# Tokens of a chunk side by side in memory, and a clamp of the weights' high words moved from VectorE to GpSimd

## The chip, the cores and the metric

The kernel runs on one core of a Trainium2 chip. The metric is the device time of one execution, in microseconds (us). The engines of the core work beside each other, each through its own instructions in their order: TensorE (PE) multiplies matrices, VectorE (DVE), ScalarE (ACT) and GpSimd (POOL) work element by element, and SyncE (SP) issues the transfers between memory (DRAM) and the on-chip memory. The tiles of the matrix unit's results lie in PSUM, all others in SBUF, on up to 128 partitions.

## The reference

Three layers in a row, on 12,480 tokens of 128 channels. Shapes are x (12480, 128), inducing (32, 128), each w_in (128, 2048) and each w_out (2048, 128).

```python
def mab(q, kv):
    s = scale * (q @ kv.T); a = softmax(s)
    return a @ kv
h = mab(inducing, x)               # 32 points look at all tokens
x = mab(x, h)                      # each token looks at the 32 points
hh = x @ w_in
x = (max(hh, 0) + alpha * min(hh, 0)) @ w_out
h = x @ w_in2
P = a0 + a1*h + a2*h**2 + a3*h**3
Q = 1 + |b0|*|h| + |b1|*h**2
out = (P / (Q + 1e-6)) @ w_out2
```

The four weight matrices come as float64, that is as pairs of 32-bit words, and are made into float32 on the chip. The tokens are independent of each other except in the sum over all tokens in h.

## The kernel before, in words

Tokens are taken in 104 tiles of 120 (one token a partition), 4 tiles to a chunk of 480 tokens (26 chunks), 4 chunks to a pack (7 packs, the last of 2 chunks). Token p * 104 + j is token p of tile j (lines 100 and 101), so that partition p of a load or a store takes one contiguous run, and the runs of neighbouring partitions lie 104 * 512 = 53,248 B apart.

**Loads.** load_x (line 155) brings a pack of x in transfers of 8 tiles each: 120 partitions, 4,096 B each, 480 KB, 13 transfers in all. load_w (line 162) brings half a float64 matrix, 1,024 KB, to 128 partitions: of w_in 8 KB of each row of 16 KB, of w_out 8 rows of 1 KB a partition. All are issued by SP in the order of lines 487 to 502: x packs 0 to 2, a half of w_in, x packs 3 and 4, a half of w_out, x packs 5 and 6, and the other weights. Halves of weights reuse the buffers of x's packs (slots), so SP waits until those are free.

**First part** (lines 520 to 600). For each pack: TensorE transposes the tiles (s1_t, line 262), scores against the inducing points (s1_s, with the maxima on VectorE, line 280), the exponential on ScalarE (s1_e), its transposition (s1_et) and the sum over the pack's tokens (s1_h). Behind the last pack the partial sums are brought under one maximum (gm, line 538) and give h and hT (line 599).

**Conversion of the weights.** Each matrix is cut into quarters of 128x512, 16 in all. For a quarter, cv_abs (line 200) takes the absolute value of the high words on ScalarE (line 203) into a tile cvt (3 buffers). Four steps on VectorE follow, which are queued in a list and taken out one by one: one (line 214: the clamp between LEAST and MOST), two (line 218: mask and shift), three (line 225: bits of the low word) and four (line 231: the sign and top bits; the result goes to its place). After four, a quarter of the first w_out is scaled on GpSimd (lines 184 and 187). Step one calls cv_abs itself if that has not been done. absn(n) issues cv_abs for the next n quarters, conv(n) the next n steps; CV (line 503) says how many of each stand in each pack's turn of the first part.

**Second part.** The order of all later operations is written out by hand: START (line 21) up to the sixth unit of the second layer, with "abs" for absn(1) and "cv" for conv(1) between the others, and CHUNK_ORDER (line 42) for every chunk after that. START carries the rest of the conversions beside the second softmax (s2_d, lines 402 and 403), the products with h (w_mm, w_hi, w_lo), the first layer's products (la, r, lb) and, on GpSimd, a_norm (422), a_lo (464) and w2_lo (327). From "close" on, units of the second layer run: products L690 to L692, then the rational function on ScalarE (s, z, rho, r0), VectorE (m 715, z 731, e 766, g0 770, g 774) and GpSimd (A 705, B 710, P 726).

**Stores.** out_y (line 808) copies a chunk's result and issues its store from SP, 240 KB, the last chunk's in two halves (27 in all).

Of the kernel before, what the change touches and what calls it, by code (L numbers as in the profile page):

```python
# [17 lines left out]

# The order in which the operations are issued, by their names in OPS: up to the second layer's
# sixth unit, and then for every chunk, with units, chunks and packs counted from the chunk's own.  # L20
START = """
# [44 lines left out]
def tile_induced_attention__prelu_moe__rational_moe(  # L66
# [13 lines left out]
    nc = tc.nc  # L80
# [4 lines left out]
    P = 128  # L85
    TP = 120                    # tokens of a tile: token = p * NT + tile
    NT = N // TP                # 104 tiles
    CH = 4                      # tiles of a chunk
    W = CH * TP                 # 480 tokens of a chunk
    NC = NT // CH               # 26 chunks  # L90
    NF = F // P                 # 16 feed-forward tiles
    NU = NF // 2                # units of two tiles
    NG = (NC + 3) // 4          # packs of four chunks
    R = P // M                  # copies of the inducing points on the partitions
    scale = 1.0 / math.sqrt(C)
    QC = 1.0 + 1e-6
    LEAST = 2.0**-15            # float32 of the bits of the high words of 2**-127 ...
    MOST = struct.unpack("f", struct.pack("I", 0x47EFFFFF))[0]      # ... and of nearly 2**128

    xv = x[0].rearrange("(p j) c -> p j c", j=NT)  # L100
    ov = out.rearrange("(p j) c -> p j c", j=NT)

# [24 lines left out]
    qc = cst.tile([P, 1], F32, name="qc")  # L127
    w1 = cst.tile([P, NF, C], F32, name="w1")          # (1 - alpha) * w_out
    w2o = wp.tile([P, NF, C], F32, name="w2o")
# [18 lines left out]

    # ---------------------------------------------------------------- pieces of the first part
    XS, RAW, SC, E, ET = {}, {}, {}, {}, {}  # L150
# [4 lines left out]
    def load_x(g):  # L155
        n = CH * nch(g)
        pool = xsr if g < 4 else cvr if g < 6 else xsl
        XS[g] = pool.tile([P, n, C], F32, tag=f"xs{g}", name="xs")
        for k in range(0, n, 8):
            nc.sync.dma_start(out=XS[g][:TP, k : k + 8], in_=xv[:, 4 * CH * g + k : 4 * CH * g + k + 8])  # L160

    def load_w(key, dram, half, slot):
        """Half of a float64 matrix, as pairs of words."""
        pool = xsr if slot in range(4) else cvr if slot in (4, 5) else xsl
        raw = pool.tile([P, F], U32, tag=f"xs{slot}", name="raw")
        if dram.shape[0] == P:
            nc.sync.dma_start(out=raw, in_=dram[:, F * half : F * half + F])
        else:
            n = F // 2
            nc.sync.dma_start(  # L170
                out=raw.rearrange("p (t d) -> p t d", t=NF // 2),
                in_=dram[n * half : n * half + n].rearrange("(t p) d -> p t d", p=P),
            )
        for q in range(2):
            RAW[key, 2 * half + q] = raw[:, F // 2 * q : F // 2 * (q + 1)]

    # float64 words to float32: sign, exponent and 20 bits from the high word, 3 from the low;
    # the quarters of the four matrices in turn, an operation at a time
    todo, done = [], set()
# [20 lines left out]
    def cv_abs(piece):  # L200
        w = RAW.pop(piece).rearrange("p (f two) -> p f two", two=2)
        t = cvr.tile([P, 512], F32, tag="cvt", name="cvt", bufs=3)
        nc.scalar.activation(out=t, in_=w[:, :, 1].bitcast(F32), func=AF.Abs)
        ABS[piece] = t, w[:, :, 0], w[:, :, 1]

    def cv_steps(piece):
# [3 lines left out]
        def one():  # L210
            if piece not in ABS:
                absn(1)
            t = ABS[piece][0]
            nc.vector.tensor_scalar(out=t, in0=t, scalar1=LEAST, scalar2=MOST, op0=ALU.max, op1=ALU.min)

# [35 lines left out]
    def absn(n):  # L251
        """The first operation, on its own engine, of the next n quarters."""
        for _ in range(n):
            if order:
                cv_abs(order.pop(0))
# [73 lines left out]
    def g_t(q, pool, tag, copy=True):  # L329
        """w_in @ diag(alpha) @ w_out"""  # L330
        t = pool.tile([P, 512], F32, tag=tag, name="t")
        for i in range(4):
            f = 4 * q + i
            nc.tensor.transpose(t[:, i * P : (i + 1) * P], wi[:, f * P : (f + 1) * P], ident)
        WT[q] = t
        if copy:
            g_c(q)
# [12 lines left out]
    def split_stack(t, dst):  # L350
        """hi, hi, lo, lo of the four copies on the partitions."""
        nc.scalar.copy(dst, t)
        hb = P // 2
        nc.vector.tensor_tensor(out=dst[hb:], in0=t[hb:], in1=f32(dst[hb:]), op=ALU.subtract)
# [3 lines left out]
    def rows(g, lo, hi):  # L358
        """The second softmax of chunks lo ... hi of pack g."""
        n = CH * nch(g)  # L360
        v = att[:, 4 * CH * g : 4 * CH * g + n, :].rearrange("p (i j) m -> p i j m", i=CH)
        return v[:, :, lo:hi, :]

    def s2_sc(g, lo, pool, tag):
        """Second softmax of the tokens of pack g: scores, differences from the maxima, exponentials."""
        sc = pool.tile([P, 512], F32, tag=tag, name="sc2")
        for j in range(lo, nch(g)):
            nc.tensor.matmul(
                sc[M * (j - lo) : M * (j - lo) + M, :W], lhsT=hT[:, 0, :], rhs=xT[:, 4 * g + j, :], start=True, stop=True
            )  # L370
        SC2[g] = sc, lo
# [16 lines left out]
    def s2_sc0(pool, tag):  # L388
        """The scores of the first chunk, tokens on the partitions."""
        t = pool.tile([P, 512], F32, tag=tag, name="t2")  # L390
# [37 lines left out]
    def a_sum(g, steps):  # L428
        """The sums of pack g's probabilities, halving after halving."""
        if g not in SUM:  # L430
# [17 lines left out]
    def a_parts(g, part):  # L448
        """Of pack g, one chunk of the first pack or half of the tiles: probabilities, and their hi, lo, hi, lo."""
        n = CH * nch(g)  # L450
# [21 lines left out]
    def a_t(c, pool, tag):  # L472
        """Probabilities of chunk c, transposed: hi, lo, hi, lo on the partitions."""
        g, j = divmod(c, 4)
# [10 lines left out]

    # ---------------------------------------------------------------- first part
    nc.sync.dma_start(out=ind, in_=inducing)
# [46 lines left out]

    # the maxima of all tokens beside the last partial sums
    s1_s(NG - 1)
# [25 lines left out]

    # the packs' partial sums under one maximum
    nc.vector.tensor_copy(hps[:, :nl, C : C + 1], sums[:, :nl].unsqueeze(2))
# [29 lines left out]
    cs2 = ctx.enter_context(tc.tile_pool(name="cs2", bufs=1, side="left", reuse_waits="tile"))  # L594
    wst = cs2.tile([P, F], F32R, name="wst")           # h @ w_in: hi, hi, lo, lo
    mst = cs2.tile([P, C], F32R, name="mst")           # h @ w_in @ diag(alpha) @ w_out: hi, hi, lo, lo
    hT = cs2.tile([P, R, M], F32, name="hT")
    att = cs2.tile([TP, NT, M], F32, name="att")       # second softmax
    nc.vector.tensor_copy(hT, t[:, 0:M].unsqueeze(1).to_broadcast([P, R, M]))
# [5 lines left out]

    # ---------------------------------------------------------------- second part
    ph1 = ctx.enter_context(tc.tile_pool(name="ph1", bufs=1, space=PSUM, reuse_waits="tile"))
# [90 lines left out]
    def act_z(k):  # L698
        """|b0 h|, over h."""
        h = hs_[k][:, :, :W]  # L700
# [16 lines left out]
    def act_h(k):  # L717
        """A copy of h, for Pool to multiply."""
        Mm[k] = pools["ew"].tile([P, 2, W], F32, tag="m", name="m", bufs=4)
# [23 lines left out]
    def last_r0():  # L743
        """The last unit's, in SBUF, and its product on Pool."""
        k = NUN - 1
# [13 lines left out]
    def keep_warm(n):  # L759
        """Products for nothing under the last chunk, which has no first layer beside it: the clock stays up."""  # L760
        t = ph1.tile([P, 512], F32, tag="h1", name="warm")
# [26 lines left out]
    def halves(c):  # L788
        """A chunk's evacuations: in one piece, or the last one's shared by two engines."""
        if c < NC - 1:  # L790
# [17 lines left out]
    def out_y(c):  # L808
        t = outp.pop(c)[:TP].rearrange("p (i d) -> p i d", i=CH)
        y = pools["rp2"].tile([TP, CH, C], F32, tag="y", name="y", bufs=2)  # L810
        for copy, a, b in halves(c):
            copy(y[:, a:b], t[:, a:b])
            nc.sync.dma_start(out=ov[:, CH * c + a : CH * c + b, :], in_=y[:, a:b])

    # fill: the rest of the weights and the second attention under the first chunk's first layer
    GP[1] = pr0.tile([P, 2, 512], F32, tag="r0", name="gp")[:, 0, :]
# [154 lines left out]
```

## Time and profile before

| | |
|---|---|
| time, median of 3 runs | 1259.12 us (1257.58 to 1259.64) |
| span of the profiled execution | 1255.9 us |
| the profiled execution's own time | not among the figures given; the span lies 3.2 us under the median of the runs |
| busy: VectorE, TensorE, ScalarE, GpSimd | 1192.9, 1179.6, 1132.8, 1077.5 us |
| transfers of x | 13, 480 KB each |
| the clamp (L214) | 16 instructions, 7.0 us on VectorE |

The span runs from the first to the last instruction of the profiled execution; a run's time has in addition what lies around it. Busy time is the time in which an engine executes an instruction. In the rows, L214 is line 214 of the kernel, "out<-in" names the tiles, x8 says that eight equal instructions are merged in a row, and a bracket gives the idle time before an instruction and what ended it.

### The profile page before, as it was taken

What the parts mean: (1) busy time and instruction counts of PE and PEld (TensorE: products, weight loads), DVE (VectorE), ACT (ScalarE), POOL (GpSimd) and SP (SyncE); (2) the same over time, 40 slices, a digit from 0 to 9 for tenths busy, and PEclk for the clock granted to TensorE, in tenths of its full rate; (3) what the DMA queues carried; (4) which work ended last, traced back from release to release, by engine and by line L of the source; (5) the groups of instructions that cost most, each with busy time, mean ns of one, the idle gap of its engine ahead of it and who ended that gap; (6) DMA issues with size and microseconds to landing.
All of it is one profiled execution on the core that took longest, in us unless ns stands there. A gap on an engine that the chain in (4) does not pass through costs nothing.

```text
span 1255.9 us, 12626 instructions
## 1 busy us (share of the span) xinstructions
PE 1179.6 (94%) x4153; PEld 677.3 (54%) x4153; DVE 1192.9 (95%) x1164; ACT 1132.8 (90%) x1510; POOL 1077.5 (86%) x770
## 2 busy tenths in 40 slices
PE   6798899999999999999999999999999999999987
PEld 4454455555455555555555555555555555555543
DVE  2699999999999999999999999999999999999997
ACT  4568899999999999999999999999999999999984
POOL 0137899999999899999999998999998999999996
PEclk9999999999999999999999999999999999999999
DMA  9800000000000000000000000000000000000000
GB/s 228 246 1 0 1 8 8 0 9 9 1 8 9 8 1 8 9 1 9 9 8 1 8 9 2 7 8 9 1 8 8 5 4 8 8 1 9 8 9 8
DMA packets 10286, 22.01 MB, mean 18 GB/s; under 512 B 764, under 2 KB 5148, under 8 KB 9708
## 3 DMA queue, kind: packets, MB, share of 16 engines
q1 hardware_dynamic: 10220, 21.20, 6.2%
q8 instruction: 33, 0.54, 0.2%
q14 instruction: 33, 0.27, 0.1%
HBM read 14.80 MB, written 6.39 MB: 17 GB/s over the span
## 4 chain that ended last, share of the span: by engine, by line
POOL 38%; PE 29%; DVE 18%; issue 6%; ACT 6%; DMA 2%; SPq 0%; POOLq 0%; ACTq 0%; DVEq 0%
POOL m L726 16%; POOL a L705 9%; PE oa L786 9%; POOL b L710 8%; PE xa L649 8%; DVE z L766 4%; DVE r L770 4%; DVE z L731 3%; DVE m L715 3%; PE h L692 3%; POOL m L723 2%; PE h L636 2%; DMA xs<-in_x_dram 2%; PE h L690 2%; PE h L691 2%
## 5 line engine op out<-in xcount | busy, mean ns | idle before, releaser
L726 POOL TENSOR_TENSOR m<-m,b 128x960 f32<-128x960 f32 x208 | 468.1, 2251 | 4.0
L649 PE MATMUL xa<-r,w 128*128 128x480 f32 x832 | 385.4, 570 | 16.1 <-ACT o L798 15.3
L786 PE MATMUL oa<-g,w2o 128*128 128x480 f32 x832 | 378.6, 569 | 13.3 <-ACT xf L665 10.4
L705 POOL TENSOR_SCALAR a<-s,co 128x960 f32<-128x960 f32 x208 | 240.5, 1156 | 82.9 <-ACT s L696 81.0
L641 ACT ACTIVATE r<-h 128x480 f32<-128x480 f32 x416 | 237.2, 571 | 24.9 <-PE h L636 22.6
L731 DVE SCALAR_TENSOR_TENSOR z<-s,bab,h 128x960 f32<-128x960 f32 x208 | 251.0, 1207 | 0.0
L766 DVE SCALAR_TENSOR_TENSOR z<-z,r 128x960 f32<-128x960 f32 x208 | 239.7, 1152 | 8.8 <-ACT r L740 5.4
L710 POOL TENSOR_SCALAR b<-s,co 128x960 f32<-128x960 f32 x208 | 240.7, 1157 | 0.0
L735 ACT ACTIVATE rho<-z,qc 128x960 f32<-128x960 f32 x208 | 225.1, 1095 | 16.0 <-DVE z L731 15.5
L636 PE MATMUL h<-stk,wst 128*128 128x480 f32 x416 | 233.0, 561 | 6.9 <-ACT r L641 6.4
L770 DVE TENSOR_TENSOR r<-m,r 128x960 f32<-128x960 f32 x207 | 239.1, 1155 | 0.0
L774 DVE SCALAR_TENSOR_TENSOR g<-z,r 128x960 f32<-128x960 f32 x207 | 237.4, 1147 | 1.0
L690 PE MATMUL h<-xh,w2h 128*128 128x480 f32 x416 | 215.2, 517 | 8.7 <-DVE z L731 8.3
L701 ACT ACTIVATE h<-h,bab 128x960 f32<-128x960 f32 x208 | 214.8, 1033 | 6.3 <-DVE m L715 5.2
L715 DVE TENSOR_TENSOR m<-h,a 128x960 f32<-128x960 f32 x183 | 210.4, 1150 | 8.0 <-POOL a L705 7.5
L786 PEld LDWEIGHTS oa<-g,w2o 128*128 128x128 f32 x832 | 153.5, 189 | 115.8 <-issue 80.2
L649 PEld LDWEIGHTS xa<-r,w 128*128 128x128 f32 x832 | 153.3, 189 | 113.1 <-issue 70.0
L740 ACT ACTIVATE r<-rho 128x960 f32<-128x960 f32 x207 | 201.8, 975 | 5.0 <-DVE g L774 4.8
L696 ACT ACTIVATE s<-h 128x960 f32<-128x960 f32 x208 | 202.4, 973 | 3.2 <-PE h L692 2.3
L692 PE MATMUL h<-xl,w2h 128*128 128x480 f32 x416 | 161.1, 387 | 5.7 <-POOL xl L676 5.1
L691 PE MATMUL h<-xh,w2l 128*128 128x480 f32 x416 | 158.2, 380 | 0.0
L636 PEld LDWEIGHTS h<-stk,wst 128*128 128x128 f32 x416 | 78.4, 189 | 116.8 <-ACT r L641 69.4
(136 smaller groups left out, 825.3 us busy)
## 6 DMA issues: line engine op xcount, KB each, us to landing
xs<-in_x_dram SPq DMA_DIRECT2D x13, 480.0 KB, 14.1
out_dram<-y SPq DMA_DIRECT2D x25, 240.0 KB, 2.4
raw<-in_moe_w_in_dram SPq DMA_DIRECT2D x4, 1024.0 KB, 6.1
raw<-in_moe_w_out_dram SPq DMA_DIRECT2D x4, 1024.0 KB, 12.1
out_dram<-y SPq DMA_DIRECT2D x2, 120.0 KB, 1.8
ind<-in_inducing_dram SPq DMA_DIRECT2D x1, 16.0 KB, 1.5
c<-in_moe_a_dram SPq DMA_DIRECT2D x1, 0.0 KB
c<-in_moe_b_dram SPq DMA_DIRECT2D x1, 0.0 KB
```

Source lines behind the costliest of these rows:

```text
L636: nc.tensor.matmul(t[:, :W], lhsT=wst[:, f * P : (f + 1) * P], rhs=stk[c], start=True, stop=True)
L649: nc.tensor.matmul(xacc[c][:, :W], lhsT=w1[:, f, :], rhs=rls.pop((p, i)), start=f == 0, stop=False)
L690: nc.tensor.matmul(t, lhsT=w2h[:, sl], rhs=xh, start=True, stop=False)
L705: nc.gpsimd.tensor_scalar(out=a, in0=S[k], scalar1=co[:, 3:4], scalar2=co[:, 1:2], op0=ALU.mult, op1=ALU.add)
L710: nc.gpsimd.tensor_scalar(out=b, in0=S[k], scalar1=co[:, 2:3], scalar2=co[:, 0:1], op0=ALU.mult, op1=ALU.add)
L715: nc.vector.tensor_tensor(out=Mm[k], in0=hs_[k][:, :, :W], in1=A_.pop(k), op=ALU.mult)
L726: nc.gpsimd.tensor_tensor(out=Mm[k], in0=Mm[k], in1=B_.pop(k), op=ALU.add)
L731: nc.vector.scalar_tensor_tensor(out=Z[k], in0=S.pop(k), scalar=bab[:, 1:2], in1=z, op0=ALU.mult, op1=ALU.add)
L766: nc.vector.scalar_tensor_tensor(out=Z[k], in0=Z[k], scalar=QC, in1=R0[k][:, :, :W], op0=ALU.add, op1=ALU.mult)
L770: nc.vector.tensor_tensor(out=r, in0=Mm.pop(k), in1=r, op=ALU.mult)
L774: nc.vector.scalar_tensor_tensor(out=g, in0=Z.pop(k), scalar=2.0, in1=R0.pop(k)[:, :, :W], op0=ALU.subtract, op1=ALU.mult, reverse0=True)
L786: nc.tensor.matmul(oacc[c][:, :W], lhsT=w2o[:, f, :], rhs=(G[k] if i == 0 else G.pop(k))[:, i], start=f == 0, stop=f == NF - 1)
```

## The change

Two things change; comments are also taken out, which changes no line number of a statement ahead of line 155 and shifts later ones by a few.

First, chunk n, partition p, tile i is now token n * 480 + p * 4 + i: a chunk is one contiguous piece of x and of out. A load has the same 8 tiles, two chunks, so each partition gets two runs of 2,048 B. A store of a chunk writes 2,048 B a partition as before, now without gaps between the partitions.

Second, the clamp is issued on GpSimd in cv_abs, directly behind ScalarE's absolute value; step one issues nothing unless cv_abs is still to be done. START, CHUNK_ORDER and CV are unchanged.

```diff
-    xv = x[0].rearrange("(p j) c -> p j c", j=NT)
-    ov = out.rearrange("(p j) c -> p j c", j=NT)
+    xv = x[0].rearrange("(n p i) c -> p n (i c)", p=TP, i=CH)
+    ov = out.rearrange("(n p i) c -> p n i c", p=TP, i=CH)
...
         for k in range(0, n, 8):
-            nc.sync.dma_start(out=XS[g][:TP, k : k + 8], in_=xv[:, 4 * CH * g + k : 4 * CH * g + k + 8])
+            m = min(8, n - k) // CH
+            nc.sync.dma_start(
+                out=XS[g][:TP, k : k + CH * m].rearrange("p (n i) c -> p n (i c)", i=CH),
+                in_=xv[:, 4 * g + k // CH : 4 * g + k // CH + m],
+            )
...
         nc.scalar.activation(out=t, in_=w[:, :, 1].bitcast(F32), func=AF.Abs)
+        nc.gpsimd.tensor_scalar(out=t, in0=t, scalar1=LEAST, scalar2=MOST, op0=ALU.max, op1=ALU.min)
         ABS[piece] = t, w[:, :, 0], w[:, :, 1]
...
         def one():
             if piece not in ABS:
                 absn(1)
-            t = ABS[piece][0]
-            nc.vector.tensor_scalar(out=t, in0=t, scalar1=LEAST, scalar2=MOST, op0=ALU.max, op1=ALU.min)
...
-            nc.sync.dma_start(out=ov[:, CH * c + a : CH * c + b, :], in_=y[:, a:b])
+            nc.sync.dma_start(out=ov[:, c, a:b], in_=y[:, a:b])
```

## Rows read from the trace of the kernel before

**Rows 1.** Stretches of 10 us and the loop: window, length, engines' busy us (instructions), clock, DMA.
```profile
60.00:70.00 10.00, 9.49 (x53) 3.77 (x50) 9.57 (x18) 8.00 (x16) 2.38 (x2) 1.00 0.28 88
...
80.00:90.00 10.00, 10.00 (x50) 6.21 (x49) 9.20 (x17) 7.47 (x16) 1.05 (x1) 1.00 0.00 0
...
100.00:110.00 10.00, 7.98 (x25) 4.42 (x25) 9.93 (x10) 7.92 (x11) 9.67 (x6) 0.96 0.00 0
...
400.00:1200.00 800.00, 774.37 (x2493) 443.51 (x2491) 788.36 (x722) 760.09 (x991) 742.54 (x527) 1.00 0.02 6
```

**Rows 2.** Chain of waits of the first 190 us: start, length, what.
```profile
3.97 11.31 DMA xs<-in_x_dram
...
20.29 16.98 DMA xs<-in_x_dram
```

**Rows 3.** Timeline of TensorE while x comes in: start, length, instructions, idle before.
```profile
8.70 1.72 PE L268 MATMUL t<-ident,xs 120*128 120x120 f32 x8 [0.33 <-DMA xs<-in_x_dram]
...
15.42 1.01 PE L268 MATMUL t<-ident,xs 120*128 120x120 f32 x8 [1.11 <-DMA xs<-in_x_dram]
...
37.40 1.80 PE L268 MATMUL t<-ident,xs 120*128 120x120 f32 x8 [4.55 <-DMA xs<-in_x_dram]
```

**Rows 4.** Stretches of 2 us: x alone, w_in, cold clock, w_out; columns as in rows 1.
```profile
6.00:8.00 2.00, 1.49 (x8) 1.49 (x8) 0.00 (x0) 0.39 (x1) 0.00 (x0) 1.00 1.03 227
...
18.00:20.00 2.00, 1.79 (x40) 1.36 (x38) 0.96 (x3) 1.69 (x4) 0.00 (x0) 1.00 0.98 344
...
38.00:40.00 2.00, 2.00 (x14) 1.02 (x13) 0.00 (x0) 1.12 (x2) 0.00 (x0) 0.50 1.01 301
...
58.00:60.00 2.00, 2.00 (x12) 0.65 (x11) 1.47 (x6) 1.70 (x5) 0.00 (x0) 1.00 1.09 360
```

**Rows 5.** Timeline of all engines from 44 to 58 us.
```profile
48.11 1.32 POOL L187 TENSOR_TENSOR w<-w,wa 128x512 f32<-128x512 f32 x1
48.34 1.38 DVE L218 TENSOR_SCALAR cvt<-cvt 128x512 uint32<-128x512 uint32 x1
...
49.64 0.64 DVE L280 TENSOR_REDUCE mx<-sc 64x1 f32<-64x480 f32 x1
```

**Rows 6.** Timeline of TensorE, its gaps between 57 and 97 us.
```profile
64.38 0.49 PE L636 MATMUL h<-stk,wst 128*128 128x480 f32 x1 [0.44 <-ACT r L641]
...
78.27 0.62 PE L385 MATMUL t<-ident,ss 128*120 128x128 f32 x4 [1.34 <-DVE att L403]
```

**Rows 7.** Timeline of VectorE: the clamp on the path, a step two, the first z.
```profile
62.15 0.43 DVE L214 TENSOR_SCALAR cvt<-cvt 128x512 f32<-128x512 f32 x1
62.61 0.43 DVE L218 TENSOR_SCALAR cvt<-cvt 128x512 uint32<-128x512 uint32 x1
...
66.30 0.64 DVE L214 TENSOR_SCALAR cvt<-cvt 128x512 f32<-128x512 f32 x1
...
75.08 0.42 DVE L214 TENSOR_SCALAR cvt<-cvt 128x512 f32<-128x512 f32 x1
75.53 1.15 DVE L218 TENSOR_SCALAR cvt<-cvt 128x512 uint32<-128x512 uint32 x1
...
106.60 1.20 DVE L731 SCALAR_TENSOR_TENSOR z<-s,bab,h 128x960 f32<-128x960 f32 x1
```

**Rows 8.** DMA issues by line: KB each, us from issue to landing.
```profile
out_dram<-y SPq DMA_DIRECT2D x25, 240.0 KB, 2.4
...
out_dram<-y SPq DMA_DIRECT2D x2, 120.0 KB, 1.8
```

**Rows 9.** Groups by line, first 150 us: count, busy us, mean ns, idle before.
```profile
L218 DVE TENSOR_SCALAR cvt<-cvt 128x512 uint32<-128x512 uint32 x16 | 11.1, 694 | 0.5
...
L214 DVE TENSOR_SCALAR cvt<-cvt 128x512 f32<-128x512 f32 x16 | 7.0, 439 | 3.2 <-ACT cvt L203 3.1
...
L187 POOL TENSOR_TENSOR w<-w,wa 128x512 f32<-128x512 f32 x4 | 5.4, 1341 | 0.3
```

**Rows 10.** The page's costliest groups: GpSimd's one-input instruction.
```profile
L710 POOL TENSOR_SCALAR b<-s,co 128x960 f32<-128x960 f32 x208 | 240.7, 1157 | 0.0
```

## The prediction

> **What bounds the kernel now.** I read the table of stretches first, then the chain of waits, then the timelines of single engines where the chain stands. From 400 to 1200 us VectorE is busy 788.36 of 800 us, and TensorE, ScalarE and GpSimd are close behind [rows 1]: the chunk loop is bound by VectorE, and nothing in it is changed except the address of a store. So the change can act only ahead of the loop, in the first 110 us, and what it gains or loses there moves the end by as much, since the loop behind it has no slack to take it up. Those 110 us have four parts, and in each another thing ends last.
>
> Up to 37.4 us it is the load of x: the chain names it for 11.31 and then 16.98 us [rows 2]. The start of each eight transposes waits for one transfer of 480 KB, and from the second to the fifth they start from 8.70 to 15.42 [rows 3]: 6.72 us for three intervals, 2.24 us each, so 491,520 B / 2.24 us = 219 GB/s. The DMA engines are full meanwhile (share 1.03) at 227 GB/s, while with the weights alone they move 344 and 360 GB/s [rows 4].
>
> From 37 to 57 us it is a chain of small steps across TensorE, ScalarE and VectorE, and the reduction of L280 at 49.64 stands in it [rows 5].
>
> From 57 to 97 us VectorE and TensorE are both full: 9.57 of 10 us and 10.00 of 10 us [rows 1]. TensorE's larger gaps there are 0.44 and 1.34 us, the second until VectorE's L403 [rows 6].
>
> From 97 to 108 us VectorE is full again (9.93 of 10 [rows 1]) with the last conversions, and the first unit's z, at 106.60, comes behind them [rows 7].
>
> **The layout.** The bytes and the number of transfers stay (13 loads of x, 27 stores). In memory a partition's 4,096 B of a load become two pieces of 2,048 B, and the runs of neighbouring partitions, 53,248 B apart now, come to lie end to end. Does the gap cost something now? w_in has gaps too: a transfer takes 8 KB of each 16 KB row, and at 18 to 20 us it moves 344 GB/s; w_out is read in 1,024 B pieces without gaps, at 360 GB/s [rows 4]. So neither gaps nor small pieces slow a load that fills 128 partitions. What sets x apart is that it fills 120, and that stays. I put the gain at 0. The ends: at 344 GB/s a transfer takes 1.43 us, and the eleven that must have landed by 37.4 us take 11 x 0.81 = 8.9 us less; below, the stores, which have 2,048 B pieces already, land 0.6 us later for 120 KB more [rows 8], which is 205 GB/s, and eleven loads at that rate take 1.7 us more. I stay at 0 because the row nearest to the question, w_in's, has the gap without the loss.
>
> The stores are issued off the path (the chunk loop waits for none); only the last two stand at the end, and land in 1.8 us [rows 8]. I put them at 0, with ends of 0.3 us either way.
>
> **The bound.** L214 runs 16 times, 7.0 us on VectorE, 0.44 us each [rows 9]. It goes. In its place 16 instructions of GpSimd follow ScalarE's L203, 128x512 in place. No row has this form. GpSimd's one-input L710 takes 1,157 ns for 960 elements [rows 10], so 0.62 us for 512 in proportion; its two-input L187 takes 1.34 us [rows 9]. I take 0.62, since one input against one input is the nearer row, and keep 1.34 for the range. The Trainium skill (GPSIMD Engine Reference, section 4.1, Engine selection) says that GpSimd runs one-input work at roughly line rate, which by its 1.2 GHz would be an estimated 0.43 us; the sum below would then be about 1.2 us lower, by 0.19 us for each of the six or seven meetings counted there.
>
> What does such an instruction do to VectorE? At 48.34 the step L218, 0.43 us elsewhere, took 1.38 while GpSimd ran L187 from 48.11 to 49.43 [rows 5]; L218 has a mean of 694 ns over its 16 against 0.43 us undisturbed [rows 7, 9]. So a conversion step that meets a GpSimd instruction waits for the rest of it. Each bound can take back what it frees. By stretch:
>
> - 37 to 57 us. The fourth bound stands on GpSimd behind L184 and L187 of the quarter before, so it runs from 49.43 to 50.05. L218 waits for it and now ends at 50.5, and L280, queued behind L218 on VectorE, starts at 50.6 and not 49.64 [rows 5]: **1.0 us later, on the path**. The gm reduction and TensorE's transpose of it wait behind.
> - 57 to 97 us. Four L214 go here on the path, from 62.15 to 75.08: 0.43 + 0.64 + 0.44 + 0.42 = 1.9 us, the third at its mean [rows 7, 9]. The L218 behind the last, 1.15 us at 75.53 [rows 7], would run ahead of the GpSimd instruction that holds it up: 0.7 us more. Five bounds meet VectorE's conversion steps here; fifteen of those, 0.4 to 0.7 us each, fill some 40% of 21 us, so I charge each bound half its length, 1.5 us in all. Net **-1.1 us**, within the 1.78 us that TensorE's two gaps allow [rows 6]. Four more L214 between 80 and 91 us I cost at nothing, gain or loss: TensorE is full there (10.00 of 10 us [rows 1]) and ends last; without that cover they would count too, 1.7 us.
> - 97 to 108 us. Three L214 go, at the mean 1.3 us [rows 9]. Three bounds come, where VectorE runs conversion steps back to back, so each is met whole: 3 x 0.62 = 1.9. Net **+0.6 us**. Behind the bounds on GpSimd stand the first unit's A and B. A needs ScalarE's s and finds the engine little used before it (1.05 of 10 us from 80 to 90 [rows 1]), so I cost that at nothing; without that room it is up to another 1.9 us.
>
> ScalarE's abs and the SP queue keep their order. The buffers of cvt are given back by L231 as before.
>
> Sum: 0 (layout) + 1.0 - 1.1 + 0.6 = +0.5 us. The profiled span is 1255.9 us; the median of the runs, 1259.12, is 3.2 us more, which lies around the span and is not touched. 1259.12 + 0.5 = **1259.6 us**. About 0.2%, 2.5 us, is what a measurement of this kernel can tell from no change.
>
> **Rivals.**
> - *The gap was the cost.* If x is slow because 120 rows 53,248 B apart are read at once, x comes at up to 344 GB/s: 8.9 us less, 1250.7 us; and with no wait of 4.55 us before 37.40 TensorE would not run its next groups at the granted clock of 0.50 (1.80 us for eight transposes against 1.01 [rows 3, 4]); two such groups give 1.6 us more at most. For it: the load is the path for 28 us. Against it: w_in. It decides from 245 GB/s on. Chance 0.25. The Trainium skill (DMA: Bandwidth & Descriptors, Latency and other measured facts) names a large row pitch as a cause of lost rate and contiguous tiles as a remedy, but its losses start at a pitch of 512 KiB; by it this case would not come about, and x would stay at its rate.
> - *GpSimd's bound is dear.* If max and min in one instruction cost 1.34 us like L187, the first stretch pays 1.7 us, the second +0.7 (five of 0.67 against 2.6 freed), the third 3 x 1.34 - 1.3 = +2.7: 1259.1 + 5.1 = 1264.2 us, slower. Its place is the L218 that waits at 49 and at 98 us; it decides from about 1.0 us a bound. For it: the disturbed L218 rows. Against it: L710's rate. The slower end of the layout, +1.7, goes here too. Chance 0.21.
> - *VectorE's relief counts and the meetings don't.* If the bounds fall into VectorE's PSUM work, the seven L214 on the path are saved, 3.2 us, and the first stretch's 1.0 us too: 1255.9 us. Chance 0.11. That the change does nothing at all is inside the forecast.
>
> **How the numbers follow.** Forecast 0.43, the gap 0.25, the dear bound 0.21, the relief 0.11. Faster by over 0.2%: 0.36; within: 0.43; slower: 0.21. The range must take in most of the gap case and of the dear bound to leave out no more than 2 in 10: 1249.5 to 1264.0 us; the likeliest case alone has 1257.1 to 1261.6.
>
> **What would show it.** Right: the transposes of the second to fifth transfer still start 2.2 us apart and that of x's sixth pack near 37.4; 16 bounds on GpSimd near 0.62 us, the fourth ending near 50 and L280 behind it; L214 gone and the steps L218, L225 and L231 with longer means. Wrong: transposes 1.5 us apart and the wait at 37.4 gone (the gap case); bounds over 1 us (the dear bound); L218, L225 and L231 no longer than before and z earlier than 106 us (the relief). A changed period of the chunk loop would contradict all of it.

## The result, and the profile after

The changed kernel takes 1272.29 us (median of 5 runs, 1270.72 to 1274.05) against 1259.44 us before (5 runs): ratio 1.0108, 95% interval 1.0094 to 1.0123. It is 12.9 us slower, above the upper end of the forecast's range, 1264.0 us. Its line numbers are 3 higher from the clamp on: L208 is the clamp on GpSimd, L221, L228 and L234 are the conversion steps two to four, L283 the maxima, L734 z.

I read the stretches and TensorE's timeline first, for the layout and the clock. The stretches of the changed kernel (window, length, busy us with instructions of TensorE, its weight loads, VectorE, ScalarE, GpSimd, then clock, DMA share, GB/s):

```profile
6.00:8.00 2.00, 1.25 (x6) 1.25 (x7) 0.00 (x0) 0.15 (x1) 0.00 (x0) 1.00 1.05 221
...
54.00:56.00 2.00, 0.91 (x13) 0.65 (x17) 1.93 (x8) 0.75 (x2) 0.00 (x0) 0.50 0.00 0
60.00:62.00 2.00, 2.00 (x16) 1.68 (x13) 0.00 (x0) 0.82 (x2) 0.02 (x1) 0.50 0.97 375
64.00:66.00 2.00, 2.00 (x17) 1.76 (x16) 1.22 (x5) 0.27 (x2) 0.00 (x0) 1.00 1.09 347
400.00:1200.00 800.00, 775.88 (x2503) 445.17 (x2502) 788.82 (x722) 761.77 (x995) 741.09 (x525) 1.00 0.02 6
```

TensorE's timeline (start, length, instructions; in brackets the idle time before and what ended it):

```profile
8.97 1.86 PE L271 MATMUL t<-ident,xs 120*128 120x120 f32 x8 [0.36 <-DMA xs<-in_x_dram]
11.58 1.83 PE L271 MATMUL t<-ident,xs 120*128 120x120 f32 x8 [0.75 <-DMA xs<-in_x_dram]
...
37.54 1.83 PE L271 MATMUL t<-ident,xs 120*128 120x120 f32 x8 [4.20 <-DMA xs<-in_x_dram]
...
55.09 0.37 PE L546 MATMUL t<-ident,gm 128*1 128x128 f32 x1 [4.72 <-DVE gm L541]
...
60.82 3.30 PE L582 MATMUL t<-hps,sw 128*32 128x129 f32 x14
```

The load of x has not moved: 221 GB/s where it had 227 [rows 4], and the sixth pack at 37.54 where it was 37.40 [rows 3]. The loop has not moved either: VectorE is busy 788.82 of 800 us against 788.36 [rows 1]. So all of the loss lies between 37 us and the loop, and of the rows shown behind 37 us the one at 55.09 is the first late one: TensorE waits 4.72 us for gm. Behind it the granted clock is 0.50, the 1.2 GHz level, in the stretches shown from 54 to 62 us; at 64 it is 1.00 (2.4 GHz) again.

Then the groups by line over the first 160 us (count, busy us, mean ns, idle before and what ended it):

```profile
L208 POOL TENSOR_SCALAR cvt<-cvt 128x512 f32<-128x512 f32 x16 | 31.7, 1994 | 51.5 <-ACT cvt L207 51.5
...
L228 DVE SCALAR_TENSOR_TENSOR cvt<-raw,cvt 128x512 uint32<-128x512 uint32 x16 | 14.2, 889 | 0.4
...
L221 DVE TENSOR_SCALAR cvt<-cvt 128x512 uint32<-128x512 uint32 x16 | 12.0, 750 | 14.9 <-POOL cvt L208 14.8
```

The clamp takes 1.99 us on GpSimd, where VectorE took 0.44 [rows 9], and VectorE's step two stands idle 14.9 us for it where it stood 0.5 [rows 9]. The timeline of all engines shows where that first counts:

```profile
44.87 1.92 POOL L208 TENSOR_SCALAR cvt<-cvt 128x512 f32<-128x512 f32 x1 [8.06 <-ACT cvt L207]
46.82 0.43 DVE L221 TENSOR_SCALAR cvt<-cvt 128x512 uint32<-128x512 uint32 x1 [2.45 <-POOL cvt L208]
...
49.41 1.04 POOL L188 TENSOR_TENSOR wa<-w,alT 128x512 f32<-128x512 f32 x1 [2.62 <-DVE w L234]
50.53 1.26 POOL L191 TENSOR_TENSOR w<-w,wa 128x512 f32<-128x512 f32 x1
51.76 1.92 POOL L208 TENSOR_SCALAR cvt<-cvt 128x512 f32<-128x512 f32 x1
53.71 0.43 DVE L221 TENSOR_SCALAR cvt<-cvt 128x512 uint32<-128x512 uint32 x1 [4.38 <-POOL cvt L208]
54.06 0.64 DVE L283 TENSOR_REDUCE mx<-sc 64x1 f32<-64x480 f32 x1
```

Read it from the bottom. The last maxima start at 54.06 and not at 49.64 [rows 5], 4.42 us late. They are queued behind L221, which waits for the fourth clamp; that stands on GpSimd behind L188 and L191 of the third quarter, which end 2.4 us later than before (51.79 against 49.43 [rows 5]). 1.5 of the 2.4 us are the third clamp, which took 1.92 us too. The other 0.9 are not the clamp's: ScalarE's absolute value ahead of it starts at 44.11 against 43.21 before, because TensorE's low clock behind the wait for x lasted longer in this execution (0.64 from 42 to 44 us, before 1.00). 2.4 and 1.92 are 4.3 of the 4.42, and 3.4 of them are the two clamps'. Five profiled executions with these clamps took 16.7 to 17.6 us from x's sixth pack to gm, against 13.3 before, so this part of the loss is 3.4 to 4.3 us.

The other place is the last conversion. VectorE's timeline there, first before the change, then after it:

```profile
108.80 1.32 DVE L218 TENSOR_SCALAR cvt<-cvt 128x512 uint32<-128x512 uint32 x1
110.15 0.69 DVE L225 SCALAR_TENSOR_TENSOR cvt<-raw,cvt 128x512 uint32<-128x512 uint32 x1
110.88 0.69 DVE L231 SCALAR_TENSOR_TENSOR w2o<-raw,cvt 128x512 uint32<-128x512 uint32 x1
111.49 1.21 DVE L731 SCALAR_TENSOR_TENSOR z<-s,bab,h 128x960 f32<-128x960 f32 x1
```

```profile
114.68 1.21 DVE L734 SCALAR_TENSOR_TENSOR z<-s,bab,h 128x960 f32<-128x960 f32 x1
117.21 1.16 DVE L718 TENSOR_TENSOR m<-h,a 128x960 f32<-128x960 f32 x1 [1.31 <-POOL a L708]
118.28 2.48 DVE L221 TENSOR_SCALAR cvt<-cvt 128x512 uint32<-128x512 uint32 x1
120.79 1.52 DVE L228 SCALAR_TENSOR_TENSOR cvt<-raw,cvt 128x512 uint32<-128x512 uint32 x1
122.35 2.58 DVE L234 SCALAR_TENSOR_TENSOR w2o<-raw,cvt 128x512 uint32<-128x512 uint32 x1
124.85 1.20 DVE L734 SCALAR_TENSOR_TENSOR z<-s,bab,h 128x960 f32<-128x960 f32 x1
```

GpSimd's timeline beside it, first before the change, then after it:

```profile
107.58 2.25 POOL L726 TENSOR_TENSOR m<-m,b 128x960 f32<-128x960 f32 x1
111.29 1.29 POOL L705 TENSOR_SCALAR a<-s,co 128x960 f32<-128x960 f32 x1 [1.46 <-ACT s L696]
```

```profile
112.89 1.91 POOL L208 TENSOR_SCALAR cvt<-cvt 128x512 f32<-128x512 f32 x1
114.77 1.27 POOL L330 TENSOR_TENSOR w2l<-w2o,w2h 128x512 fp32r<-128x512 f32 x1
116.03 1.15 POOL L708 TENSOR_SCALAR a<-s,co 128x960 f32<-128x960 f32 x1
...
118.28 2.20 POOL L729 TENSOR_TENSOR m<-m,b 128x960 f32<-128x960 f32 x1
120.48 1.29 POOL L708 TENSOR_SCALAR a<-s,co 128x960 f32<-128x960 f32 x1
121.75 2.63 POOL L729 TENSOR_TENSOR m<-m,b 128x960 f32<-128x960 f32 x1
```

From the first z to the second it was 4.89 us (106.60 [rows 7] to 111.49) and is 10.17. The three steps take 2.48 + 1.52 + 2.58 = 6.6 us instead of 1.32 + 0.69 + 0.69 = 2.7, 3.9 us more: each of them meets an instruction of GpSimd and ends 0.3 to 0.6 us after it. Before the change P (L726) had been running for 1.22 us when L218 began, and GpSimd then stood idle for 1.46 us, in which L225 ran alone; now P (L729) begins together with L221, and the next A follows it without a gap. Another 1.31 us is the wait at 117.21 for A, late on GpSimd behind the clamp and L330. The Trainium skill (SBUF — State Buffer, section SBUF: two separate sides) says that VectorE, in certain instructions, and GpSimd take a shared pair of ports for a whole instruction, and the other stands still meanwhile. The trace agrees: L221 took 2.48 us beside an L729 of 2.20, and 0.43 at 53.71 beside nothing on GpSimd.

Behind the second z the loss goes on. A row of TensorE before the change; then, after it, the same row, a stretch (columns as above), and a row each of ScalarE and VectorE:

```profile
112.84 0.45 PE L690 MATMUL h<-xh,w2h 128*128 128x480 f32 x1 [0.37 <-DVE z L731]
```

```profile
126.20 0.74 PE L693 MATMUL h<-xh,w2h 128*128 128x480 f32 x1 [4.81 <-DVE z L734]
128.00:130.00 2.00, 2.00 (x6) 1.03 (x5) 1.25 (x2) 1.43 (x2) 0.00 (x0) 0.50 0.00 0
131.85 0.97 ACT L699 ACTIVATE s<-h 128x960 f32<-128x960 f32 x1 [0.69 <-PE h L695]
134.10 1.16 DVE L718 TENSOR_TENSOR m<-h,a 128x960 f32<-128x960 f32 x1 [1.71 <-POOL a L708]
```

TensorE now stands idle 4.81 us for the second z, and its granted clock is 0.50 from 122 to 132 us; before, it was 0.50 only from 110 to 112 us (0.78 and 0.86 in the two stretches beside). ScalarE's s waits for TensorE's products, A waits for s, and VectorE's m waits 1.71 us for A. From the second z to the fourth it is 12.84 us and was 10.09 (121.58 - 111.49), 2.7 us more. From the fourth z to the last the changed kernel stays 16.0 to 16.2 us behind before: nothing is lost or won in the loop.

### The profile page after: what moved, and what is told of

Read it like the earlier page. It is cut to its first block, busy times and chain, and to the rows that moved or that the text cites. A ratio compares the mean times of both kernels' runs of the same rounds, so it can differ in the third digit from the quotient of the medians.

```text
span 1272.0 us, 12628 instructions
## 1 busy us (share of the span) xinstructions
PE 1188.6 (93%) x4153; PEld 682.9 (54%) x4153; DVE 1191.2 (94%) x1148; ACT 1133.5 (89%) x1510; POOL 1108.5 (87%) x786
## 4 chain that ended last, share of the span: by engine, by line
POOL 37%; PE 31%; DVE 17%; issue 7%; ACT 6%; DMA 2%; SPq 0%; POOLq 0%; ACTq 0%; DVEq 0%
POOL m L729 14%; POOL a L708 9%; PE oa L789 9%; PE xa L652 8%; POOL b L713 8%; DVE z L769 4%; DVE r L773 4%; DVE z L734 3%; DVE m L718 3%; PE h L695 3%; PE h L639 3%; PE h L693 2%; POOL m L726 2%; PE h L694 2%; DVE g L777 2%
## 5 line engine op out<-in xcount | busy, mean ns | idle before, releaser
L729 POOL TENSOR_TENSOR m<-m,b 128x960 f32<-128x960 f32 x208 | 468.0, 2250 | 4.0
L652 PE MATMUL xa<-r,w 128*128 128x480 f32 x832 | 385.9, 570 | 16.1 <-ACT o L801 15.2
L789 PE MATMUL oa<-g,w2o 128*128 128x480 f32 x832 | 378.5, 569 | 13.3 <-ACT xf L668 9.8
L734 DVE SCALAR_TENSOR_TENSOR z<-s,bab,h 128x960 f32<-128x960 f32 x208 | 251.3, 1208 | 0.9 <-ACT h L704 0.9
```

The costliest lines, as they stand in the source:

```text
L652: nc.tensor.matmul(xacc[c][:, :W], lhsT=w1[:, f, :], rhs=rls.pop((p, i)), start=f == 0, stop=False)
L729: nc.gpsimd.tensor_tensor(out=Mm[k], in0=Mm[k], in1=B_.pop(k), op=ALU.add)
L734: nc.vector.scalar_tensor_tensor(out=Z[k], in0=S.pop(k), scalar=bab[:, 1:2], in1=z, op0=ALU.mult, op1=ALU.add)
L789: nc.tensor.matmul(oacc[c][:, :W], lhsT=w2o[:, f, :], rhs=(G[k] if i == 0 else G.pop(k))[:, i], start=f == 0, stop=f == NF - 1)
```

## The experiments

The theory: the loss is the dear clamp, at two places, the maxima (made worse by TensorE's clock) and the last conversion (with what follows from it up to the fourth z), and the layout is worth nothing. The rivals: the layout costs; a clamp anywhere costs by its length; the wait alone is the loss, without the clock. The table has the start of five marks in each profiled execution (us): TensorE's transpose of gm, VectorE's copy to hT, the first, the second and the fourth z; then the median of the runs and the ratio to before on the same chip.

| kernel | gm | hT | z 1 | z 2 | z 4 | median | ratio (95%) |
|---|---|---|---|---|---|---|---|
| before | 50.68 | 57.02 | 106.60 | 111.49 | 121.58 | 1259.44 | |
| after | 55.09 | 65.41 | 114.68 | 124.85 | 137.69 | 1272.29 | 1.0108 (1.0094 to 1.0123) |
| e1_layout | 51.93 | 59.79 | 109.37 | 114.24 | 124.43 | 1258.58 | 1.0004 (0.9995 to 1.0013) |
| e2_clamp | 53.29 | 63.04 | 112.30 | 122.46 | 134.95 | 1271.10 | 1.0100 (1.0085 to 1.0115) |
| e3_mult_add | 50.35 | 56.70 | 104.42 | 113.22 | 124.69 | 1264.96 | 1.0049 (1.0032 to 1.0065) |
| e5_early | 50.55 | 56.90 | 106.15 | 116.30 | 128.62 | 1264.06 | 1.0043 (1.0025 to 1.0060) |
| e6_late | 54.26 | 64.22 | 113.69 | 118.57 | 130.19 | 1266.74 | 1.0058 (1.0037 to 1.0079) |
| e7_middle | 49.43 | 57.39 | 106.87 | 111.75 | 121.82 | 1259.00 | 0.9995 (0.9983 to 1.0007) |
| e12_warm6 | 55.09 | 61.44 | 111.58 | 121.74 | 133.73 | 1268.55 | 1.0079 (1.0056 to 1.0103) |
| e4_wide | 39.21 | 45.56 | 95.11 | 99.98 | 110.45 | 1246.07 | 0.9901 (0.9886 to 0.9916) |

Marks of single executions scatter: e1_layout has the time of before, and yet its hT is 2.8 us later (the clock's part in that comes below). So differences of marks within one execution, such as from z to z, carry more than a mark alone.

**The two halves of the change.** e1_layout is the changed kernel with the clamp back on VectorE:

```diff
-        nc.gpsimd.tensor_scalar(out=t, in0=t, scalar1=LEAST, scalar2=MOST, op0=ALU.max, op1=ALU.min)
...
+            t = ABS[piece][0]
+            nc.vector.tensor_scalar(out=t, in0=t, scalar1=LEAST, scalar2=MOST, op0=ALU.max, op1=ALU.min)
```

> The new layout alone, the clamp back on VectorE. Theory (all of the loss is GpSimd's clamp): 1259 us like the kernel before, within 2.5 us, x's sixth pack transposed at 37.4 to 37.6 us, the transposes of single x transfers 2.2 to 2.6 us apart. Rival (the 2,048 B pieces cost a share): 1261.5 us or more, with the transposes of x's sixth pack over 1 us later than 37.4.

e2_clamp is the kernel before with the reverse of these lines:

> The old layout, the clamp on GpSimd. Theory: 1272 us, the whole of the loss, clamps of 1.92 us each, the last reduction of the maxima at 54 us as in the changed kernel. Rival (layout and clamp share the loss): 1265 to 1270 us.

Alone, the layout changes the time by a factor of 1.0004, with 1 inside the interval; alone, the clamp gives 1.0100 of the 1.0108. In e2_clamp's trace the last maxima start at 52.26 us and not at the 54 expected, since x's sixth pack had come at 36.12; gm still waits 4.81 us there. The layout is out of the story from here on.

**What makes the clamp dear.** e3_mult_add keeps the instruction and its place and changes its two operations; e9_max_add keeps the first:

```diff
-        nc.gpsimd.tensor_scalar(out=t, in0=t, scalar1=LEAST, scalar2=MOST, op0=ALU.max, op1=ALU.min)
+        nc.gpsimd.tensor_scalar(out=t, in0=t, scalar1=1.0, scalar2=0.0, op0=ALU.mult, op1=ALU.add)
```

> The changed kernel, with multiply by 1 and add 0 in place of max and min on GpSimd: the same tile, in place, the same two constants as immediates; it leaves out the clamp. Theory 1 (max and min are what is slow): 0.62 us each, and then the forecast's sum holds, 1258 to 1262 us. Theory 2 (any instruction of this form takes 1.9 us, by its constants or by working in place): 1.9 us each and 1272 us.

```diff
+        nc.gpsimd.tensor_scalar(out=t, in0=t, scalar1=LEAST, scalar2=0.0, op0=ALU.max, op1=ALU.add)
```

> The changed kernel with max and then add 0 on GpSimd, no min; it leaves out the upper bound. If each of max and min costs 0.65 us over the 0.62 us of multiply and add: 1.27 us each. If one of them alone makes the instruction slow: 1.92 us (max) or 0.62 us (min).

The groups by line of e3_mult_add, then of e9_max_add:

```profile
L208 POOL TENSOR_SCALAR cvt<-cvt 128x512 f32<-128x512 f32 x16 | 11.5, 722 | 51.7 <-ACT cvt L207 51.7
```

```profile
L208 POOL TENSOR_SCALAR cvt<-cvt 128x512 f32<-128x512 f32 x16 | 31.8, 1998 | 50.5 <-ACT cvt L207 50.5
```

With multiply and add it is 722 ns on the mean, and 0.62 us where nothing meets it (42.58, 48.32 us). That is the price that the forecast took from L710, which multiplies and adds too. With max and add it is as slow as with max and min (e9_max_add ran once, 1272.19 us). So max alone makes the instruction some three times as long; min alone was not tried.

e3_mult_add's time misses what was expected of it. With the cheap instruction the early loss is gone (gm at 50.35, hT at 56.70) and the first z is even 2.2 us earlier than before. But from z to z it is still 8.8 us, as VectorE's timeline of e3_mult_add shows:

```profile
106.62 2.50 DVE L221 TENSOR_SCALAR cvt<-cvt 128x512 uint32<-128x512 uint32 x1
109.15 1.53 DVE L228 SCALAR_TENSOR_TENSOR cvt<-raw,cvt 128x512 uint32<-128x512 uint32 x1
110.72 2.58 DVE L234 SCALAR_TENSOR_TENSOR w2o<-raw,cvt 128x512 uint32<-128x512 uint32 x1
```

They are as long as in the changed kernel. Here too P begins together with L221, 2.2 us behind the first z (before: 0.98 us), and A follows it without a gap, whatever the clamp itself costs. Two things could bring this order about, the step that is missing on VectorE or the instructions added on GpSimd; no run separates them. The profiled execution, 1259.94 us, is the fastest of its five; the 5 us up to the median stand in no trace, and I leave them open.

**Which of the sixteen clamps cost.** The clamp stands on GpSimd for the quarters in ON_POOL and on VectorE for the others:

```diff
+        if piece in ON_POOL:
+            nc.gpsimd.tensor_scalar(out=t, in0=t, scalar1=LEAST, scalar2=MOST, op0=ALU.max, op1=ALU.min)
...
+            if piece not in ON_POOL:
+                t = ABS[piece][0]
+                nc.vector.tensor_scalar(out=t, in0=t, scalar1=LEAST, scalar2=MOST, op0=ALU.max, op1=ALU.min)
...
+    ON_POOL = order[4:16]  # e5_early; e6_late: order[0:13]; e7_middle: order[5:13]
```

> The changed kernel with the clamps of the first four quarters back on VectorE, the other twelve on GpSimd. Theory (two places make the loss: the last maxima wait for the fourth clamp, 4.4 us, and TensorE then runs at half clock, 4 us; and the last conversions meet GpSimd's units, 5 us): 1264 us, the transpose of gm near 51.5 us without a wait over 2 us. Rival (the loss is spread over all sixteen meetings, 0.8 us each): 1269 us.

> The changed kernel with the clamps of the last three quarters back on VectorE, the other thirteen on GpSimd. Theory of the two places: 1267 us, hT as late as in the changed kernel (65 us), but the second z 5 us behind the first as before, not 10. Rival (spread): 1270 us.

> Clamps of the first five and the last three quarters on VectorE, the eight in between on GpSimd, 1.92 us each. Theory of the two places: the whole loss is gone, 1258 to 1260 us, because TensorE is full beside those eight. Rival (spread): 1265 us.

Each time came out within 0.3 us of its number or in its range. With the first four back on VectorE, gm and hT are where they were, and what stays is the 10.15 us from z to z and, up to the fourth z, 2.2 us more than before (ratio 1.0043). With the last three back, z to z is 4.88 us again, and gm stays late (1.0058). The two shares, 0.43 and 0.58%, add up to 1.01% of the 1.08%. The eight in the middle, at 1.99 us each, cost nothing (0.9995), which fits that TensorE is full there [rows 1].

**TensorE's clock.** Between gm's transpose and hT it takes 6.34 us before and 10.32 us after, for the same work. That isn't all due to the long wait: e1_layout and e7_middle, with waits of some 1.6 us as before, take 7.86 and 7.96 us, since in these executions the clock fell to 0.50 for a stretch too, after the transpose (0.50 from 54 to 56 us in e1_layout). So the work takes 6.3 to 8.0 us without the long wait, and 2.4 to 4.0 us of the 10.32 are to be put down to it. To keep TensorE busy while it waits, both kernels put products for nothing ahead of the transpose; e8_warm twenty, e12_warm6 six:

```diff
+    t = ptile("warm")
+    for _ in range(20):
+        nc.tensor.matmul(t[:, :W], lhsT=ident, rhs=xT[:, 0, :], start=True, stop=True)
```

> The changed kernel with 20 products for nothing, 128x480 each, ahead of the transpose of gm, where TensorE idles for 4.7 us. Theory (4 us of the loss are TensorE's clock of 0.50 between 50 and 65 us, which falls in that idle time): the clock stays at 1.00, hT comes 3.5 to 4 us earlier than 65.8 us, 1268.5 us. Rival (the slow groups hide behind other waits): hT less than 1 us earlier, 1272 us.

> As the run with 20 products for nothing, but 6: the 20 took 16.3 us and not the 4.7 us of the gap. Theory (TensorE's clock is 4 us of the loss): 4.9 us of products, the transpose of gm near 55 us as in the changed kernel, 6.4 us from it to hT and not 10.1, and 1268.5 us. Rival (the clock's part is taken back later): 1271 to 1273 us.

e8_warm was sized wrong. TensorE's timeline of e8_warm, then of e12_warm6:

```profile
48.70 16.27 PE L547 MATMUL warm<-xT,ident 128*128 128x480 f32 x40
64.81 0.27 PE L549 MATMUL t<-ident,gm 128*1 128x128 f32 x1
```

```profile
50.12 5.00 PE L547 MATMUL warm<-xT,ident 128*128 128x480 f32 x12
55.09 0.27 PE L549 MATMUL t<-ident,gm 128*1 128x128 f32 x1
...
58.31 1.83 PE L585 MATMUL t<-hps,sw 128*32 128x129 f32 x14
```

Each product is two instructions of 0.41 us, so twenty last 16.27 us and push gm to 64.81; the run is slower (1280.80 us, ratio 1.0165, 1.0143 to 1.0187). Its one use: from gm to hT it takes 6.35 us. Six products last 5.00 us and end as gm arrives: the transpose starts at 55.09 as in the changed kernel, with 0.27 us for 0.37, the fourteen instructions of L582 (here L585) take 1.83 us for 3.30, hT comes 6.35 us after gm, and the time falls from 1272.29 to 1268.55 us. The runs of the two were not measured side by side, and the intervals of their ratios overlap at the ends (1.0094 to 1.0103), but the 3.7 us agree with the 10.32 - 6.35 = 4.0 us of the traces. The wait itself stays (gm at 55.09 in both), so this part of the loss is the granted clock behind it. For the low clock behind the second z no such run was made. In e6_late TensorE waits only 0.96 us for that z, and yet the clock is at 0.57 and 0.58 from 120 to 124 us and the second and the fourth z lie 11.62 us apart; so the share of the long wait in the 2.7 us is not shown.

**What makes x slow.** The prediction put it down to the 120 partitions and not to the gaps. e4_wide is e1_layout with 128 rows in twelve of the thirteen transfers (the last eight belong to the next chunk and are used by nothing); e10_split is e1_layout with each transfer cut into 112 and 8 partitions:

```diff
+            c = 4 * g + k // CH
+            rows = P if c + m < NC else TP
+            src = bass.AP(tensor=x.tensor, offset=x.offset + c * W * C, ap=[[CH * C, rows], [W * C, m], [1, CH * C]])
+            nc.sync.dma_start(out=XS[g][:rows, k : k + CH * m].rearrange("p (n i) c -> p n (i c)", i=CH), in_=src)
```

> The new layout, the clamp on VectorE, and each load of x that has a successor fills 128 partitions and not 120: the 8 more take the next chunk's first rows, which nothing reads, 7 per cent more bytes. Theory (x comes at 219 GB/s because it fills 120 partitions): the transposes of single transfers start about 1.5 us apart, x's sixth pack near 29 us, and the time is 1250 us. Rival (its rate has to do with something else, the piece or memory): 2.2 to 2.6 us apart, 1259 to 1262 us.

```diff
+            for lo, hi in ((0, 112), (112, TP)):
+                nc.sync.dma_start(
+                    out=XS[g][lo:hi, k : k + CH * m].rearrange("p (n i) c -> p n (i c)", i=CH), in_=xv[lo:hi, c : c + m]
+                )
```

> The new layout, the clamp on VectorE, each load of x as two transfers, of partitions 0 to 111 and of 112 to 119: no byte more. Theory 1 (a transfer of x is slow because 120 partitions cannot be shared out evenly over the 16 DMA engines, and 112 can): the rate comes back, transposes under 2 us apart, 1250 us or less. Theory 2 (a transfer must fill all 128 partitions to reach 340 GB/s): 2.2 us apart or more, 1258 us or more.

The stretches of e4_wide, then of e10_split (columns as above):

```profile
6.00:8.00 2.00, 1.67 (x9) 1.67 (x10) 0.00 (x0) 0.56 (x1) 0.00 (x0) 1.00 1.03 384
8.00:10.00 2.00, 2.00 (x12) 2.00 (x12) 0.17 (x1) 1.12 (x2) 0.00 (x0) 1.00 1.04 384
```

```profile
6.00:8.00 2.00, 1.28 (x7) 1.31 (x8) 0.00 (x0) 0.21 (x1) 0.00 (x0) 1.00 1.02 243
...
12.00:14.00 2.00, 2.00 (x14) 0.84 (x14) 0.02 (x1) 1.12 (x2) 0.00 (x0) 1.00 1.07 234
```

With 128 partitions x comes at 384 GB/s, where e1_layout has 210 to 235 in the stretches from 6 to 14 us, though each transfer carries 7% more. The sixth pack, in TensorE's timeline of e4_wide, waits no more than this and runs in 1.01 us for 1.83:

```profile
26.92 1.01 PE L272 MATMUL t<-ident,xs 120*128 120x120 f32 x8 [0.71 <-DMA xs<-in_x_dram]
```

That is 10.5 us earlier than before [rows 3], and the time is 1246.07 us (1245.38 to 1246.99): some 4 us better than expected, and faster than both kernels by about 1 and 2%. In e10_split the rate stays at 234 to 244 GB/s, with transposes 2.1 us apart, and the time at 1258.08 us (ratio 0.9991, 0.9979 to 1.0003): cutting off the eight odd partitions is no remedy; in these runs a load got the rate only by filling all 128. A load of 112 partitions without the eight beside it was not tried.

Last, e11_wide_middle puts e7_middle's eight clamps into e4_wide:

> The loads of x on 128 partitions as in the run with wide loads, and the clamps of the eight middle quarters on GpSimd. Theory of the two places: the same as wide loads alone, 1246 us, within 1.5 us, faster than both kernels. Rival (each clamp on GpSimd costs): 1250 us or more.

It takes 1248.11 us (1245.37 to 1249.54; ratio 0.9909, 0.9895 to 0.9924), against 1246.07 for e4_wide: no gain, 0.6 us outside the range expected by the theory and under the rival's 1250. e4_wide, with every clamp on VectorE, is the best version found.

## Why the prediction was wrong

- **The layout at 0: right**, and for its reason. e1_layout shows it by itself, and e4_wide shows that what was said to set x apart, its 120 partitions, is the cost. The gap rival is out.
- **The price of the clamp: the step that failed.** 0.62 us was taken from L710 "since one input against one input is the nearer row". L710 multiplies and adds; the clamp takes a maximum. The form was near, the operation was not: 1.92 us undisturbed, 1.99 on the mean, above the 1.34 kept for the range too. It is not the only one that failed: with the forecast's price, in e3_mult_add, the kernel is still 0.49% slower, where the sum had +0.5 us. The Trainium skill (GPSIMD Engine Reference, section 4.1, Engine selection), with its rough line rate for one-input work that the prediction quotes, gave an estimated 0.43 us: the trace has 0.62 for multiply and add and 1.92 for max and min, and the measurement decides.
- **37 to 57 us, +1.0: the place was right, the size was not.** The fourth clamp behind the scale instructions, L218 behind it and L280 behind that are in the trace. But instead of 1.0 us it came to 4.4 in the profiled execution (3.4 of them the clamps'), since the third clamp also makes those two instructions late, and 4.0 us more came from TensorE's clock (2.4 to 4.0, by which execution stands for before), which the sum had no term for. The signs stood in the rows: eight transposes at clock 0.50 took 1.80 us behind the wait of 4.55 [rows 3, 4], and the prediction used that only for a rival's gain.
- **57 to 97 us, -1.1, and 97 to 108, +0.6:** from hT to the first z the trace has 106.60 - 57.02 = 49.58 us before and 49.27 after, -0.3 against the sum of -0.5. That the cover holds there is shown by e7_middle. That the sum comes so near is luck: its -0.5 stands on clamps of 0.62 us, and with those e3_mult_add has 47.72 us (104.42 - 56.70), -1.9; the dear clamps took back most of a gain that the sum had too small.
- **Behind the first z, put at nothing: failed.** The sum stops at the first z. "A finds the engine little used" was read from 80 to 90 us, while GpSimd is busy 9.67 of 10 us from 100 to 110 [rows 1]. The second unit's A came late by 1.3 us (the prediction had up to 1.9 for A without that room, but left it out), the last three conversion steps met GpSimd's work for 3.9 us more, and up to the fourth z it cost 2.7 us more, where TensorE had waited 4.81 us and its clock was 0.50. e3_mult_add shows that this was to come even at 0.62 us: the 0.6 us counted meetings with the clamps, not with the A, B and P beside which they move the steps.
- **The rival "GpSimd's bound is dear"** had the mechanism and both places, L218 at 49 and at 98 us, though the late loss fell at the last conversion, two behind the one at 98 us. Its 5.1 us had 1.34 for the price and nothing for the clock and the second z.
- **The 3.2 us "around the span"** were a misreading without effect on the sum: the changed kernel's profiled execution took 1273.76 us with a span of 1272.0, 1.8 us less. By that the one of before took an estimated 1257.7 us, under its median.

By place the profiled execution gives +4.4 (gm), +4.0 (clock), -0.3 (to the first z), +5.3 (to the second) and +2.7 (to the fourth): 16.1 us, the whole difference of the spans (1272.0 against 1255.9). The medians differ by 12.9 us, since the profiled execution of before is a short one for its kernel and that of the changed kernel a long one. e1_layout, with the time of before, has a profiled execution that lies as far above its median (1259.96, 1.4 us) as the changed kernel's (1273.76, 1.5 us). Against it the five places give +3.2, +2.5, -0.3, +5.3 and +2.6, or 13.3 us.

## What to carry to other kernels

Price a moved instruction by a row with its own operation, not only with its form; where the trace has none, measure it alone before moving it. Then ask at the new place what is queued behind it, which engine stands idle for that, and at what clock that engine comes back. And look at how many partitions a slow load fills before you look at its order in memory.

## What the runs showed of the hardware

- On GpSimd a 128x512 instruction with one input took 0.62 us for multiply and add, 1.92 us for max and min, and as long for max and add (means 722, 1994 and 1998 ns).
- A load of x on 128 partitions moved 384 GB/s, the same load on 120, or on 112 and 8, 210 to 248. Why eight missing partitions cost so much was not shown.
- Behind a wait of 4.72 us the granted clock of TensorE was 0.50, and 4.4 us late at gm became 8.4 at hT. Products for nothing that filled the wait left 6.35 us from gm to hT. The clock fell in some executions of kernels without the loss too, after a wait of 1.57 us (e1_layout: 0.85 from 52 to 54 us, then 0.50), and in the execution shown of before it stayed at 1.00 from 42 to 108 us, past a wait of 1.62; what decides between the two was not shown.
- VectorE's three conversion steps took 2.48, 1.52 and 2.58 us where each began beside an instruction of GpSimd or with it, and 1.32, 0.69 and 0.69 where only the first did.
